# Cross network on one core: state kept as a factor, last bias added on the way to the rows, row buffer shared with the second x buffer

## The chip, the cores and the metric

The kernel runs on one core of a Trainium2 chip. The metric is the device time of one execution in microseconds; the median of three runs of the kernel before is 131.28 (131.22 to 131.41). Times inside a run come from one profiled execution and count from its span's start.

The engines that matter are TensorE (PE, matrix products into PSUM), VectorE (DVE, elementwise work), ScalarE (ACT, evictions from PSUM with a bias or as a copy) and SyncE (SP), whose in-order queue issues nearly all transfers. Each engine runs its own list of instructions in order and waits on semaphores of the others.

## The reference

```python
B, F, D, L = 4096, 26, 16, 6
Din = min(F * D, 1024)          # 416
x0: [4096, 416] bf16, ws: [6, 416, 416] bf16, bs: [6, 416] bf16

def reference(x0, ws, bs):
    x = x0
    for l in range(ws.shape[0]):
        x = x0 * (x @ ws[l] + bs[l]) + x
    return x
```

Each of the six layers multiplies the state by a 416x416 matrix, adds a bias, multiplies elementwise by the input and adds the state.

## The kernel before

The state is held transposed: features on partitions, batch rows along the free dimension. 416 features are three blocks of 128 (index k or m, tiles `XM[0]`, `XM[1]`, `XM[2]` of 128 x 3 x 4096) and a remainder of 32 (`XR[0]` to `XR[2]`, packed so that the four groups of 512 rows lie in four bands of 32 partitions). The batch is two halves, s = 0 and 1, of 2048 rows, each of four groups g of 512. `XM[0]` and `XR[0]` hold x0 through the whole kernel; the other two buffers of each kind take turns as the state read (`cur`) and written (`nxt`).

Start: x0 is loaded transposed by eight DMAs (`load_x0t`), weights and small pieces follow, and `X0rows` takes x0 again with batch rows on partitions. `bias_setup` transposes the biases into `bM` and `bR`, a value for each partition.

Layer 0 is `first_layer(s)`. Layers 1 to 4 are the loop over l: for six tiles (s, m), taken in pairs, `mm_full` and `mm_row` give a tile of 128 x 2048 in two PSUM buffers (h = 0 and 1, 1024 columns each); `rem_pair` does the remainder columns after the first pair. The elementwise work of a 128 x 1024 part is `ew_main`: ScalarE evicts with the bias (L165), VectorE multiplies by x0 (L166) and adds the old state (L169). `ew_rem` does the same with 512 columns (L173 to L175). PSUM has four buffers of two banks; `tpool` has six buffers t between ScalarE and VectorE.

The last layer (l = 5) is computed the other way round, with batch rows on partitions, so that the output is written as it lies in memory. Its products take the transposed state as the stationary operand, and its elementwise work needs x0 and the state in rows. For this, layer 4 issues DMA transposes on SyncE's queue: `xl_dmat(s, k)` right after each of its six tiles (L205, into `XLrows`), and one for each half of the remainder (L274, into `scrR`), which ScalarE then copies into `XLrows` (`xl_rem`, L278).

The last stage handles eight row blocks (`quads`) in four rounds of two; rounds 1 and 2 are s = 0, rounds 3 and 4 are s = 1. In a round TensorE makes eight units of 128 x 416: `mm_q_full` (three products a unit, L327), `mm_q_rem` (the remainder's product, L333, and the bias as a product of a row of ones with the bias row `bLr`, L336). `ew` evicts a unit or a pair of units by a copy on ScalarE (L354), multiplies by `X0rows` on VectorE (L355), and puts the pair's sum with `XLrows` off until the next call (`close_sum`, L344), after which the output transfer is issued (L345). So VectorE alternates between the product of one unit and the sum of the unit before:

```python
        tc.keep_in_program_order(nc.vector.tensor_tensor(out=tv, in0=tv, in1=X0rows[:, b, :], op=ALU.mult))
        close_sum()
        pending.append((o[:, 0:n, :], tv, XLrows[:, b, :], out_v[:, b, :], eng))
```

The order of each engine's list is settled when the program is built: the Tile scheduler may move instructions by its own estimate, except those under `keep_in_program_order`; semaphore waits are derived from which tile's region is read or written.

Of the kernel before, what the change touches and what calls it, by code (L numbers as in the profile page):

```python
# [10 lines left out]
ALU = mybir.AluOpType  # L11
# [5 lines left out]
def kernel(  # L17
# [33 lines left out]
    ones = const.tile([P, P], BF16)  # L51
# [4 lines left out]
    bLr = const.tile([P, D], BF16)  # L56
# [3 lines left out]
    XLrows = big.tile([P, NBT, D], BF16)  # L60
# [4 lines left out]
    XM = [big.tile([P, NK, B], BF16, name=f"XM{i}") for i in range(3)]  # L65
    XR = [big.tile([P, NS * CW], BF16, name=f"XR{i}") for i in range(3)]

# [29 lines left out]
    nc.gpsimd.memset(ones[:], 1.0)  # L97
# [28 lines left out]
    for g in range(NG):  # L126
        nc.sync.dma_start(bLr[32 * g:32 * g + 1, :], bs[LL:LL + 1, :])
# [18 lines left out]
    def bias_setup():  # L146
# [6 lines left out]
        nc.vector.tensor_copy(bR[:], pb[:, 3, 0:L])  # L153

# [7 lines left out]
    def ew_main(l, s, m, h, pt, cur, nxt, pin=False):  # L162
        c0 = col0(s, 2 * h)
        t = tpool.tile([P, 2 * CW], BF16, name="t")
        nc.scalar.activation(t[:], pt[:].rearrange("p a b -> p (a b)"), ACT.Identity, bias=bM[:, m, l:l + 1], scale=1.0)  # L165
        prod = nc.vector.tensor_tensor(out=t[:], in0=t[:], in1=XM[0][:, m, c0:c0 + 2 * CW], op=ALU.mult)  # L166
        if pin:
            tc.keep_in_program_order(prod)
        nc.vector.tensor_tensor(out=nxt[:, m, c0:c0 + 2 * CW], in0=t[:], in1=cur[:, m, c0:c0 + 2 * CW], op=ALU.add)  # L169

    def ew_rem(l, s, pr, curR, nxtR):
        tr = tpool.tile([P, 2 * CW], BF16, name="t")
        nc.scalar.activation(tr[:, 0:CW], pr, ACT.Identity, bias=bR[:, l:l + 1], scale=1.0)  # L173
        nc.vector.tensor_tensor(out=tr[:, 0:CW], in0=tr[:, 0:CW], in1=XR[0][:, CW * s:CW * s + CW], op=ALU.mult)  # L174
        nc.vector.tensor_tensor(out=nxtR[:, CW * s:CW * s + CW], in0=tr[:, 0:CW], in1=curR[:, CW * s:CW * s + CW], op=ALU.add)  # L175

    def mm_full(l, s, m, g, pts, cur, first, last):
        c0 = col0(s, g)
        for k in range(NK):
            for q in range(4):  # L180
                nc.tensor.matmul(pts[g // 2][32 * q:32 * q + 32, g % 2, :], lhsT=WM[:, l, k, 128 * m + 32 * q:128 * m + 32 * q + 32],  # L181
                                 rhs=cur[:, k, c0:c0 + CW], start=(first and k == 0), stop=(last and k == NK - 1),
# [8 lines left out]
    def mm_rem(l, s, pr, cur, curR):  # L191
# [3 lines left out]
        for k in range(NK):  # L195
            for g in range(NG):
                c0 = col0(s, g)
                nc.tensor.matmul(pr[32 * g:32 * g + 32, :], lhsT=WM[:, l, k, NK * P:D], rhs=cur[:, k, c0:c0 + CW],  # L198
                      start=False, stop=(k == NK - 1), tile_position=(0, 32 * g))
# [4 lines left out]
    def xl_dmat(s, k, nxt):  # L204
        nc.sync.dma_start_transpose(out=XLrows[:, 16 * s:16 * s + 16, 128 * k:128 * k + 128],  # L205
                                    in_=nxt[:, k, SW * s:SW * s + SW])

    def first_layer(s):
        cur, curR, nxt, nxtR = XM[0], XR[0], XM[1], XR[1]

        def full(pt, m, h, gl, after_row):
            c0 = col0(s, 2 * h + gl)
            for k in range(NK):
                nc.tensor.matmul(pt[:, gl, :], lhsT=WM[:, 0, k, 128 * m:128 * m + 128], rhs=cur[:, k, c0:c0 + CW],  # L214
# [30 lines left out]
        for m in range(NK):  # L245
            ew_main(0, s, m, 0, pa[m], cur, nxt)
# [11 lines left out]
        for m in range(NK):  # L258
            ew_main(0, s, m, 1, pb[m], cur, nxt, pin=(s == 0))
        ew_rem(0, s, pr[:, 0, :], curR, nxtR)  # L260
# [6 lines left out]
    def rem_pair(l, cur, curR, nxtR, feeds_last):  # L267
# [3 lines left out]
        for s in range(NS):  # L271
            ew_rem(l, s, pr2[:, s, :], curR, nxtR)
            if feeds_last:
                nc.sync.dma_start_transpose(out=scrR[s][:], in_=nxtR[:, CW * s:CW * s + CW])  # L274

    def xl_rem(s):
        tc.keep_in_program_order(
            nc.scalar.copy(XLrows[:, 16 * s:16 * s + 16, NK * P:D].rearrange("p (g i) r -> p i g r", g=NG),  # L278
                           scrR[s][:].rearrange("p i (g r) -> p i g r", g=NG)))

    cur, curR = XM[1], XR[1]
    for l in range(1, LL):
        nxt, nxtR = XM[1 + (l % 2)], XR[1 + (l % 2)]
# [129 lines left out]
```

## Time and profile before

| what | value |
| --- | --- |
| median of three runs | 131.28 us (131.22 to 131.41) |
| profiled execution: span | 128.9 us (no total of its own is given) |
| mean granted TensorE clock | 0.998 |
| layer 0, TensorE from 12.14 to 26.9 us | TensorE busy 14.86 of 14.90, VectorE 13.86, ScalarE 11.10 (12.1 to 27.0) |
| layers 1 to 4, 27.0 to 103.85 us | TensorE busy 76.85 of 76.85, VectorE 70.20, ScalarE 55.66 |
| layer 4 alone, 84.60 to 103.85 us | TensorE busy 19.25 of 19.25, VectorE 17.33, ScalarE 14.29 |
| last stage to 115.8 us (11.95 us) | TensorE busy 11.95, VectorE 10.90, ScalarE 8.50 |
| 115.8 us to the end (13.10 us) | TensorE busy 8.74, VectorE 10.10, ScalarE 7.94 |
| L165, eviction 128x1024 | 48 in layers 1 to 4, 1.115 us each |
| L166 and L169, VectorE 128x1024 | 60 each, 0.690 and 0.696 us |
| L355 and L344, VectorE 128x832 | 9 each, 0.589 and 0.584 us |
| L355 and L344, VectorE 128x416 | 14 each, 0.367 and 0.366 us |
| output transfers of 208 KB, of 104 KB | 9 and 14; 2.4 and 1.7 us from issue to landing (median) |

A busy time is the union of an engine's instructions in the stretch. Matrix products are pipelined, so a single one's duration (379 ns for 512 columns) is longer than the distance between two starts; the chain of waits gives the time that a group takes on the path.

### The profile page before, as it was taken

The numbers are of one execution on the slowest core, as the hardware profiler recorded it, in microseconds if no ns is written. First come the engines' busy times: TensorE is split into PE (matmuls) and PEld (weight loads), VectorE is DVE, ScalarE is ACT, GpSimd is POOL, SyncE is SP. The second block draws the span as 40 slices with busy tenths as digits, with TensorE's granted clock in tenths as the row PEclk, the third lists the DMA queues.
The fourth block names the chain that finished last, engine by engine and source line by source line (L and its number), as shares of the span: only waits on it lengthen the run. The fifth ranks groups of instructions, "written<-read, shape, count | busy, mean of one in ns | idle before, by whom it ended". The sixth has DMA issues, their size and how long they took to land.

```text
span 128.9 us, 3973 instructions
## 1 busy us (share of the span) xinstructions
PE 123.1 (96%) x1690; PEld 54.9 (43%) x1690; DVE 107.1 (83%) x197; ACT 86.9 (67%) x99; POOL 5.9 (5%) x18
## 2 busy tenths in 40 slices
PE   6999999999999999999999999999999999999960
PEld 2343443354444444444444444444444445445420
DVE  1032979999999898989898989898989899898991
ACT  0426783987848577848668848668847896569670
POOL 4022200600000000000000000000000000000000
PEclk9999999999999999999999999999999999999999
DMA  3999999999990000000000000000297999995754
GB/s 106 237 203 217 170 158 260 247 328 333 336 299 11 5 0 8 0 0 5 0 5 0 5 0 5 0 5 0 42 166 164 123 219 178 187 323 188 231 179 139
DMA packets 42102, 16.37 MB, mean 127 GB/s; under 512 B 30906, under 2 KB 42084, under 8 KB 42084
## 3 DMA queue, kind: packets, MB, share of 16 engines
q1 hardware_dynamic: 39416, 15.56, 54.6%
q10 hardware_dynamic: 2668, 0.56, 2.3%
q8 instruction: 13, 0.21, 0.7%
q14 instruction: 5, 0.04, 0.1%
HBM read 6.15 MB, written 3.41 MB: 74 GB/s over the span
## 4 chain that ended last, share of the span: by engine, by line
PE 80%; DMA 8%; DVE 5%; issue 2%; SPq 1%; ACT 1%; DVEq 0%
PE pt L181 49%; PE ph L214 9%; DMA XM<-in_x_dram 8%; PE py L327 8%; PE pt L187 5%; PE pr L198 5%; DVE t L355 3%; DVE o L344 2%; PE pr L193 2%; SPq L76 1%; PE py L333 1%; PE ph L221 1%; PE py L336 1%; ACT t L354 1%; PE pr L157 0%
## 5 line engine op out<-in xcount | busy, mean ns | idle before, releaser
L181 PE MATMUL pt<-XM,WM 128*32 128x512 bf16 x1152 | 65.2, 379 | 0.0
L165 ACT ACTIVATE t<-pt,bM 128x1024 bf16<-128x1024 f32 x48 | 49.6, 1115 | 18.3 <-PE pt L187 18.3
L166 DVE TENSOR_TENSOR t<-t,XM 128x1024 bf16<-128x1024 bf16 x60 | 41.4, 690 | 5.3 <-ACT t L165 5.3
L169 DVE TENSOR_TENSOR XM<-t,XM 128x1024 bf16<-128x1024 bf16 x60 | 41.8, 696 | 3.4
L181 PEld LDWEIGHTS <-WM 128*32 128x32 bf16 x1152 | 29.7, 97 | 33.8 <-issue 5.1
L354 ACT CAST t<-py 128x416 bf16<-128x416 f32 (+1 forms) x23 | 14.8, 642 | 4.8 <-PE py L327 2.1
L327 PE MATMUL py<-WM,XM 128*128 128x416 bf16 x96 | 17.7, 340 | 0.0
L214 PE MATMUL ph<-XM,WM 128*128 128x512 bf16 x72 | 16.5, 379 | 0.1
L165 ACT ACTIVATE t<-ph,bM 128x1024 bf16<-128x1024 f32 x12 | 12.5, 1114 | 4.4 <-PE ph L221 4.4
L327 PEld LDWEIGHTS <-XM 128*128 128x128 bf16 x96 | 9.0, 98 | 8.5 <-issue 1.4
L355 DVE TENSOR_TENSOR t<-t,X0rows 128x416 bf16<-128x416 bf16 (+1 forms) x23 | 10.4, 454 | 1.2 <-ACT t L354 1.2
L214 PEld LDWEIGHTS <-WM 128*128 128x128 bf16 x72 | 6.8, 98 | 8.6 <-issue 1.3
L344 DVE TENSOR_TENSOR o<-t,XLrows 128x416 bf16<-128x416 bf16 (+1 forms) x23 | 10.3, 451 | 0.0
L173 ACT ACTIVATE t<-pr,bR 128x512 bf16<-128x512 f32 x10 | 6.4, 684 | 2.7 <-PE pr L198 2.1
L198 PE MATMUL pr<-XM,WM 128*32 128x512 bf16 x120 | 8.2, 379 | 0.0
L187 PE MATMUL pt<-XR,WR 32*128 32x512 bf16 x96 | 7.3, 379 | 0.0
L141 PE MATMUL wps<-warm 128*128 128x512 bf16 (+1 forms) x11 | 4.4, 593 | 1.2 <-DVE warm L94 1.2
L175 DVE TENSOR_TENSOR XR<-t,XR 128x512 bf16<-128x512 bf16 x10 | 4.2, 423 | 0.7
L198 PEld LDWEIGHTS <-WM 128*32 128x32 bf16 x120 | 3.2, 97 | 3.1
L106 ACT ACT_TABLE_LOAD x1 | 1.3, 1283 | 4.3 <-DMA WM<-in_ws_dram 4.3
L174 DVE TENSOR_TENSOR t<-t,XR 128x512 bf16<-128x512 bf16 x10 | 4.2, 418 | 0.0
L152 DVE CAST bM<-pb 128x18 f32<-128x18 bf16 x1 | 0.2, 177 | 4.6 <-PE pb L151 4.6
(39 smaller groups left out, 33.6 us busy)
## 6 DMA issues: line engine op xcount, KB each, us to landing
X0rows<-in_x_dram SPq DMA_DIRECT2D x4, 832.0 KB, 11.6
out_dram<-o SPq DMA_DIRECT2D x9, 208.0 KB, 2.4
WM<-in_ws_dram SPq DMA_DIRECT2D x5, 312.0 KB
out_dram<-o SPq DMA_DIRECT2D x13, 104.0 KB, 1.7
WR<-in_ws_dram SPq DMA_DIRECT2D x4, 130.0 KB, 4.1
WM<-in_ws_dram ACTq DMA_DIRECT2D x1, 312.0 KB
XM<-in_x_dram SPq DMA_TRANSPOSE x8, 4.9
xrig<-in_x_dram ACTq DMA_DIRECT2D x4, 32.0 KB, 4.1
```

Source lines behind the costliest of these rows:

```text
L165: nc.scalar.activation(t[:], pt[:].rearrange("p a b -> p (a b)"), ACT.Identity, bias=bM[:, m, l:l + 1], scale=1.0)
L166: prod = nc.vector.tensor_tensor(out=t[:], in0=t[:], in1=XM[0][:, m, c0:c0 + 2 * CW], op=ALU.mult)
L169: nc.vector.tensor_tensor(out=nxt[:, m, c0:c0 + 2 * CW], in0=t[:], in1=cur[:, m, c0:c0 + 2 * CW], op=ALU.add)
L173: nc.scalar.activation(tr[:, 0:CW], pr, ACT.Identity, bias=bR[:, l:l + 1], scale=1.0)
L181: nc.tensor.matmul(pts[g // 2][32 * q:32 * q + 32, g % 2, :], lhsT=WM[:, l, k, 128 * m + 32 * q:128 * m + 32 * q + 32], rhs=cur[:, k, c0:c ...
L187: nc.tensor.matmul(pts[g // 2][:, g % 2, :], lhsT=WR[32 * g:32 * g + 32, l, 128 * m:128 * m + 128], rhs=curR[32 * g:32 * g + 32, CW * s:CW ...
L198: nc.tensor.matmul(pr[32 * g:32 * g + 32, :], lhsT=WM[:, l, k, NK * P:D], rhs=cur[:, k, c0:c0 + CW], start=False, stop=(k == NK - 1), tile ...
L214: nc.tensor.matmul(pt[:, gl, :], lhsT=WM[:, 0, k, 128 * m:128 * m + 128], rhs=cur[:, k, c0:c0 + CW], start=(k == 0 and not after_row), sto ...
L327: nc.tensor.matmul(py[:, 0:D], lhsT=cur[:, k, q_cols(q, g)], rhs=WM[:, l, k, :], start=((not closes) and k == 0), stop=(closes and k == NK ...
L344: tc.keep_in_program_order(nc.vector.tensor_tensor(out=o, in0=t, in1=xl, op=ALU.add))
L354: nc.scalar.copy(tv, src)
L355: tc.keep_in_program_order(nc.vector.tensor_tensor(out=tv, in0=tv, in1=X0rows[:, b, :], op=ALU.mult))
```

## The change

The state is kept as a factor c with x = x0 * c, so that one layer is c <- c + (x @ W + b), x <- x0 * c. The factor lies in new tiles `CM` and `CR`. In layer 0 c is 1 + (x0 @ W + b): the eviction writes it directly with a bias that has 1 added (`bias_setup`), and VectorE only multiplies. In layers 1 to 4 VectorE adds the evicted t to c and multiplies c by x0.

The rows needed by the last stage are now those of c with the last layer's bias already added: out = x0 * ((x @ W) + (c + b)). So the last stage adds the rows of c first and multiplies by `X0rows` second (`ew`, `close_out`), and the products of ones with `bLr` are gone, with `ones`, `bLr` and its four loads. The bias is added to the transposed c, in place, 1024 columns at a time: six parts on ScalarE (the set `ON_ACT`, issued by `act_bias`) and six on VectorE, the remainder's two parts on VectorE.

The rows of c are written into `shared[s]`, one tile for each half, which also serves as the second x buffer (`x2_cols`) in place of `XM[2]`. Layer 4 reads x from it. `XLrows` is gone. `cl_dmat`, the transpose into `shared[s]`, is issued for (0,0) and (0,1) after the tile (0,2), for (0,2) after the tile (1,0), for (1,0) at the end of layer 4, and for (1,1) and (1,2) in the source after the second pair of rounds 1 and 2.

In the compiled program SyncE's queue has, in this order: two remainder transposes; `shared[0]` k = 0, 1, 2; `shared[1]` k = 0, 1; four output transfers; `shared[1]` k = 2; the other output transfers. The first row addition waits for the three transposes of `shared[0]`, the first of s = 1 for the three of `shared[1]`.

```diff
-    ones = const.tile([P, P], BF16)
-    bLr = const.tile([P, D], BF16)
-    XLrows = big.tile([P, NBT, D], BF16)
-    XM = [big.tile([P, NK, B], BF16, name=f"XM{i}") for i in range(3)]
+    XM = [big.tile([P, NK, B], BF16, name=f"XM{i}") for i in range(2)]
+    CM = big.tile([P, NK, B], BF16)
+    shared = [big.tile([P, 16, D], BF16, name=f"shared{s}") for s in range(NS)]
     XR = [big.tile([P, NS * CW], BF16, name=f"XR{i}") for i in range(3)]
+    CR = big.tile([P, NS * CW], BF16)
...
+    def x2_cols(k, s, c, n):
+        return shared[s][:].rearrange("p b d -> p (b d)")[:, SW * k + c:SW * k + c + n]
+
+    XC = [x0_cols, x1_cols, x2_cols]
...
-    for g in range(NG):
-        nc.sync.dma_start(bLr[32 * g:32 * g + 1, :], bs[LL:LL + 1, :])
...
+        nc.vector.tensor_scalar_add(bM[:, :, 0:1], bM[:, :, 0:1], 1.0)
+        nc.vector.tensor_scalar_add(bR[:, 0:1], bR[:, 0:1], 1.0)
...
+    def ew_main(l, s, m, h, pt, nxt, pin=False):
         c0 = col0(s, 2 * h)
+        c = CM[:, m, c0:c0 + 2 * CW]
+        if l == 0:
+            nc.scalar.activation(c, pt[:].rearrange("p a b -> p (a b)"), ACT.Identity, bias=bM[:, m, 0:1], scale=1.0)
+        else:
+            t = tpool.tile([P, 2 * CW], BF16, name="t")
+            nc.scalar.activation(t[:], pt[:].rearrange("p a b -> p (a b)"), ACT.Identity, bias=bM[:, m, l:l + 1], scale=1.0)
+            nc.vector.tensor_tensor(out=c, in0=t[:], in1=c, op=ALU.add)
+        prod = nc.vector.tensor_tensor(out=nxt(m, s, 2 * h * CW, 2 * CW), in0=c, in1=XM[0][:, m, c0:c0 + 2 * CW], op=ALU.mult)
...
+    def add_last_bias(s, m, h, eng):
+        c0 = col0(s, 2 * h)
+        c, b = CM[:, m, c0:c0 + 2 * CW], bM[:, m, LL:L]
+        if eng is nc.scalar:
+            return nc.scalar.activation(c, c, ACT.Identity, bias=b, scale=1.0)
+        return eng.tensor_scalar_add(c, c, b)
...
+    def cl_dmat(s, k):
+        nc.sync.dma_start_transpose(out=shared[s][:, :, 128 * k:128 * k + 128], in_=CM[:, k, SW * s:SW * s + SW])
...
             if feeds_last:
-                nc.sync.dma_start_transpose(out=scrR[s][:], in_=nxtR[:, CW * s:CW * s + CW])
+                cs = slice(CW * s, CW * s + CW)
+                nc.vector.tensor_scalar_add(CR[:, cs], CR[:, cs], bR[:, LL:L])
+                nc.sync.dma_start_transpose(out=scrR[s][:], in_=CR[:, cs])
...
+    ON_ACT = {(0, 0, 0), (0, 2, 0), (0, 2, 1), (1, 0, 0), (1, 1, 0), (1, 2, 0)}
+
+    def act_bias(*units):
+        for u in units:
+            tc.keep_in_program_order(add_last_bias(*u, nc.scalar))
...
             for h in range(2):
-                ew_main(l, s, m, h, pts[t][h], cur, nxt)
-            if feeds_last:
-                xl_dmat(s, m, nxt)
+                ew_main(l, s, m, h, pts[t][h], nxt)
+                if feeds_last and (s, m, h) not in ON_ACT:
+                    add_last_bias(s, m, h, nc.vector)
...
             finish(ta)
+            if feeds_last and n == 2:
+                cl_dmat(0, 0)
+                cl_dmat(0, 1)
             for g in range(NG):
                 mm_full(l, tb[0], tb[1], g, pts[tb], cur, False, True)
             finish(tb)
+            if feeds_last and n == 0:
+                act_bias((0, 0, 0))
+            if feeds_last and n == 2:
+                act_bias((0, 2, 0), (0, 2, 1))
+                cl_dmat(0, 2)
+            if feeds_last and n == 4:
+                act_bias((1, 0, 0))
+                cl_dmat(1, 0)
...
-        for g in range(NG):
-            nc.tensor.matmul(py[g][:, 0:D], lhsT=ones[32 * g:32 * g + 1, :],
-                             rhs=bLr[32 * g:32 * g + 1, :], start=False, stop=(g < done), tile_position=(32 * g, 0))
...
-            tc.keep_in_program_order(nc.vector.tensor_tensor(out=o, in0=t, in1=xl, op=ALU.add))
+            tc.keep_in_program_order(nc.vector.tensor_tensor(out=o, in0=t, in1=xr, op=ALU.mult))
...
-        tc.keep_in_program_order(nc.vector.tensor_tensor(out=tv, in0=tv, in1=X0rows[:, b, :], op=ALU.mult))
-        close_sum()
-        pending.append((o[:, 0:n, :], tv, XLrows[:, b, :], out_v[:, b, :], eng))
+        tc.keep_in_program_order(nc.vector.tensor_tensor(out=tv, in0=tv, in1=shared[s][:, r, :], op=ALU.add))
+        close_out()
+        pending.append((o[:, 0:n, :], tv, X0rows[:, b, :], out_v[:, b, :], eng))
...
             ew(q + u // 4, u % 4, n, tiles[tl][:, a:a + n, 0:D], nc.scalar if q + 2 == NQ and u == 7 else nc.sync)
+            if q < 4 and u == 2:
+                act_bias((1, 1 + q // 2, 0))
+                cl_dmat(1, 1 + q // 2)
```

More of the change, by code (lines that the diff above doesn't have):

```diff
@@ L167, in ew_main, with ew_rem @@
         if pin:
             tc.keep_in_program_order(prod)
[L169 to L175, printed above, removed]
+    def ew_rem(l, s, pr, nxtR):
+        cs = slice(CW * s, CW * s + CW)
+        c = CR[:, cs]
+        if l == 0:
+            nc.scalar.activation(c, pr, ACT.Identity, bias=bR[:, 0:1], scale=1.0)
+        else:
+            tr = tpool.tile([P, 2 * CW], BF16, name="t")
+            nc.scalar.activation(tr[:, 0:CW], pr, ACT.Identity, bias=bR[:, l:l + 1], scale=1.0)
+            nc.vector.tensor_tensor(out=c, in0=tr[:, 0:CW], in1=c, op=ALU.add)
+        nc.vector.tensor_tensor(out=nxtR[:, cs], in0=c, in1=XR[0][:, cs], op=ALU.mult)
@@ L181, in mm_full @@
                 nc.tensor.matmul(pts[g // 2][32 * q:32 * q + 32, g % 2, :], lhsT=WM[:, l, k, 128 * m + 32 * q:128 * m + 32 * q + 32],
-                                 rhs=cur[:, k, c0:c0 + CW], start=(first and k == 0), stop=(last and k == NK - 1),
+                                 rhs=cur(k, s, CW * g, CW), start=(first and k == 0), stop=(last and k == NK - 1),
                                  tile_position=(0, 32 * q))
@@ L350, in ew @@
         b = slice(b0, b0 + 4 * (n - 1) + 1, 4)
+        r = slice(4 * g0 + i, 4 * (g0 + n - 1) + i + 1, 4)
         t = tpool.tile([P, 2 * CW], BF16, name="t")
@@ L381 @@
                 close(u - 1, 2)
-    close_sum()
+    close_out()
 _INS = ['x0', 'ws', 'bs']
```

49 lines of the change are left out of this document (20 added, 29 removed).

## The prediction

> **What bounds the kernel now.** I read the page's busy times and its chain first, then the waits and the timeline of the last 25 us.
>
> ```profile
> PE 123.1 (96%) x1690; PEld 54.9 (43%) x1690; DVE 107.1 (83%) x197; ACT 86.9 (67%) x99; POOL 5.9 (5%) x18
> PE 80%; DMA 8%; DVE 5%; issue 2%; SPq 1%; ACT 1%; DVEq 0%
> L336 PE MATMUL py<-bLr,ones 1*128 1x416 bf16 x32 | 2.8, 335 | 0.0
> ```
>
> TensorE is busy from 12.14 us, when its last input lands, to 115.6; there the chain passes to ScalarE and then VectorE until 126.04. So the five matrix layers are TensorE's, and the last stage is shared. That stage begins at 103.85 and has four rounds of two row blocks. TensorE takes 5.15 us for each of the first two rounds.
>
> VectorE reads as follows in the timeline where the second half of the batch (s=1) begins:
>
> ```profile
> 115.68 0.58 DVE L344 TENSOR_TENSOR o<-t,XLrows 128x832 bf16<-128x832 bf16 x1
> 116.69 0.59 DVE L355 TENSOR_TENSOR t<-t,X0rows 128x832 bf16<-128x832 bf16 x1 [0.43 <-ACT t L354]
> 117.20 0.58 DVE L344 TENSOR_TENSOR o<-t,XLrows 128x832 bf16<-128x832 bf16 x1
> 117.70 0.37 DVE L355 TENSOR_TENSOR t<-t,X0rows 128x416 bf16<-128x416 bf16 x1
> ```
>
> Operations on 128x832 start 0.50 apart and those on 128x416 0.29 apart. From 116.69 on VectorE waits for nothing long; its last sum ends at 126.32, 9.63 us later, and the span ends 2.6 us after that. Whatever moves the instruction of 116.69 moves the end.
>
> The third view is SyncE's queue, which issues the transposes of the last layer's state into rows:
>
> ```profile
> 98.83 1.22 SPq L274 DMA_TRANSPOSE scrR<-XR  x1
> 100.14 2.02 SPq L205 DMA_TRANSPOSE XLrows<-XM  x1
> 102.26 3.67 SPq L205 DMA_TRANSPOSE XLrows<-XM  x1
> 106.02 1.81 SPq L205 DMA_TRANSPOSE XLrows<-XM  x1
> 107.93 3.62 SPq L205 DMA_TRANSPOSE XLrows<-XM  x1
> 111.64 0.55 SPq L345 DMA_DIRECT2D out_dram<-o  x1
> ```
>
> Four transposes of 128x2048 one behind the other hold the queue for 2.02, 3.67, 1.81 and 3.62 us. By the trace's landing events they land 5.28, 5.04, 5.41 and 5.18 us after their issue began: at 105.4, 107.3, 111.4 and 113.1. The last is 3.6 us ahead of 116.69, so none is felt now.
>
> **The change, part by part.** All sums are against this execution (span 128.9; no total of its own is given). The median of the three runs, 131.28, lies 2.35 above the span, and I carry that over.
>
> *Taken from TensorE:* 32 products with ones. Four run side by side in 0.18 us in the chain (0.18 PE py L336 x4), so 8 x 0.18 = 1.44 us. Only the first two rounds' share, 0.72, lies ahead of 116.69; behind it VectorE sets the pace, not TensorE.
>
> *Taken from VectorE:* in layer 0 twelve additions of 128x1024 (0.70 each) and two of 128x512 (0.42), 9.2 us. They lie beside TensorE, which is never late for them between 12.14 and 26.9, so I price this at nothing. Were TensorE's cover gone they would be worth up to 9.2. Layers 1 to 4 keep two operations for each tile. The four loads of the bias row, issued between 31 and 35 us, have nothing behind them until 91.6: nothing. The two additions of 1 to the bias tiles stand behind casts that ended at 6.2, and ScalarE needs them at 11.09: nothing.
>
> *Added to ScalarE:* six in-place bias additions of 128x1024. The eviction of that shape from PSUM takes 1.115; 128x512 takes 0.684 from PSUM and 0.625 as a copy in SBUF, so 1.06 to 1.12. I take 1.08.
>
> *Added to VectorE:* six in-place additions of a per-partition bias on 128x1024 and two on 128x512. No such operation is in the trace. Above, it is bounded by the two-tensor operation of the same size, 0.69; below, by the one-tensor copy of half the size, 0.42 (L160, 128x512). I take 0.42, since the addition reads one tensor where the product reads two, and keep 0.69 for the range. Each delays what follows by about 0.46: 0.34 until the next start (operations overlap by 0.08) and 0.12 because it must see its predecessor end (0.73 instead of 0.61 between starts). The Trainium skill, VectorE: DVE Perf Modes (the perf-mode tier table), states that a one-source bf16 operation in SBUF runs four elements a cycle, a two-source one two. Estimated from its cycle breakdown that gives 0.43 for 1024; the 0.69 of L166 agrees with its rate for two sources, and no row here shows one source. By that page the sum stays as it is.
>
> *Moved:* the rows of the state now land in the buffer that the last matrix layer still reads. In the compiled order of SyncE's queue the two remainder transposes come first, then three transposes for s=0, two for s=1, four output transfers, and only then the last transpose for s=1. The row addition, which was the second operation of each pair, is now the first, and waits for all three transposes of its half. Behind a waiting addition stand all later VectorE operations, then the outputs on SyncE's queue, then ScalarE's evictions (six t buffers), then TensorE's banks.
>
> So the path is this.
> - Remainders: before, their first VectorE operation starts at 94.24. Three bias operations ahead of it add 3 x 0.46: 95.6. The first remainder with its bias is done at 97.0, the second transpose (1.23 us of queue each) has been issued at 99.5.
> - Five transposes back to back, at the durations of the fence, start at 99.5, 101.6, 105.3, 107.2 and 110.9; the queue is free at 112.9. What else they need is earlier: TensorE's last read of s=0 at 94.8 and of s=1 at 103.85; ScalarE's biases at 101.4, 106.9 and 110.2, counted on from its eviction that ends at 99.3.
> - The third lands at 105.3 + 5.2 = 110.5. VectorE, through with layer 4 at 107.57 before, gets there at about 109.7, because of the biases; so the first row addition starts at 110.6, **first wait** 0.9.
> - From it to the end of the fourth output product are nine operations, 8 x 0.505 + 0.58: 115.2. The fourth output transfer takes the queue for 0.45, so the last transpose is issued at 115.7. Its bias on ScalarE, behind the sixth eviction, is ready at about 115.3, so both ways agree. It lands at 115.7 + 5.2 = 120.9.
> - VectorE has finished s=0 at about 117.7 and waits 3.3, **second wait**, for the first addition of s=1 at 121.0 instead of 116.69: 4.3 later. The 9.63 behind it stay: VectorE is back to back there, and after a wait of that length its input is stocked.
>
> 131.28 + 4.3 = 135.6.
>
> **Rivals.**
> *Only ScalarE's chain holds (shorter).* If VectorE isn't late, because biases cost nearly nothing and the transposes keep out of each other's way, the last transpose still waits for its bias. The sixth eviction, at 112.18, starts at most 0.72 earlier: 111.46 + 0.85 + 1.08 = 113.4, landing 118.6, so 2.0 later: 133.2. Even with no change on ScalarE at all the transpose stands behind the fourth output, whose product ended at 112.63 before. For it: gaps of 0.2 to 0.4 in VectorE's layer 4 soak up a part. Against it: four transposes in a row did hold the queue 11 us.
> *Dearer.* Biases at 0.69 add 0.27 three times ahead of the remainders and twice more in their small form, about 1.0 in all, to 136.6; four output transfers in the same queue (2.4 us to landing each) may hold the last transpose 0.5 more: 137.1.
> *Faster.* The last stage follows TensorE: the rows of s=1 are there by 115.9 and the 0.72 arrives, 130.6. It decides if the last transpose is issued before 110.7. Four outputs stand ahead of it in the compiled order, the fourth of which went out at 113.32 before; against it by 2.6 us. A landing between 116 and 117 would be no change.
> *TensorE's clock drops.* In this trace the filler products L141 start 0.43 apart at the kernel's beginning, later products of that size 0.216. If the wait let the clock fall to that half, the last seven units, 0.54 each, would take 1.08 against VectorE's 0.575: 7 x 0.5 = 3.5 more, 139. The page shows a granted clock of 9 tenths or more in every slice; t buffers and banks let TensorE run on for about half of the 3.3, so it would idle less than 2. The Trainium skill, TensorE: Matmul & The Clock Gate (Part 1), puts the drop at an idle window of about 3.4 us; by that rule it doesn't come here, and no run yet shows an idle stretch so long.
> *That the change doesn't do what it says:* the compiled orders show the 32 products and 14 additions gone, so I leave that out.
>
> **How the numbers follow.** Forecast 135.6 with both waits: 0.60. Shorter, around 133.2: 0.19. Dearer, around 137: 0.10. Clock: 0.03. Faster: 0.05. No change: 0.03. A measurement of this kernel tells about 0.2% (0.26 us) from no change. Hence faster 0.05, same 0.03, slower 0.92. The range reaches from the shorter case, 133.0, to the bounds of the bias price and the crowded queue, 137.3; what it leaves out is the faster, same and clock cases and the edges of two others, under 0.2.
>
> **What would show it.** Right: L336 gone; layer 0 with one VectorE operation for each tile; the last transpose issued behind the fourth output near 115.7; and two idle stretches of VectorE ahead of the row addition, put down to a DMA, one near 110 and a longer one ending near 121; from there 9.6 us to the last product. Wrong: a last transpose that lands before 117, or a bias operation far from 0.42, or VectorE entering the last stage by 108.

## The result, and the profile after

The changed kernel takes 135.0 us (median of 4 runs, 134.66 to 135.24); the kernel before takes 131.25 beside it on the same chip (4 runs, 130.63 to 131.41). The ratio is 1.030, with a 95% interval of 1.0266 to 1.0334: 3.75 us slower. The profiled execution took 135.07 with a span of 133.2. One run of early_two_queues, 321.9 us long, counts as slow and is left out of its figure below.

From the profile of the changed kernel: its busy times, its chain by engine and the two new kinds of bias addition (busy us, mean ns of one, idle time before):

```profile
PE 122.6 (92%) x1656; PEld 54.7 (41%) x1658; DVE 102.1 (77%) x193; ACT 92.4 (69%) x105; POOL 4.9 (4%) x17
PE 63%; DVE 16%; DMA 8%; ACT 6%; issue 3%; SPq 1%; DVEq 0%; ACTq 0%
L200 ACT ACTIVATE CM<-CM,bM 128x1024 bf16<-128x1024 bf16 x6 | 7.0, 1159 | 0.3 <-DVE XM L181 0.2
L201 DVE TENSOR_SCALAR CM<-CM,bM 128x1024 bf16<-128x1024 bf16 x6 | 2.9, 486 | 0.2
```

VectorE has five microseconds less to do than before and the kernel is slower. The chain shows why that is no contradiction: TensorE's share fell from 80% to 63%, and VectorE's rose from 5% to 16%. The saved work lay in layer 0, beside TensorE; the added work lies at the end of layer 4, and there VectorE and ScalarE take the chain over.

The timeline of VectorE in the changed kernel, from its last bias addition to the first row addition of s = 1 (start, duration):

```profile
110.46 0.49 DVE L201 TENSOR_SCALAR CM<-CM,bM 128x1024 bf16<-128x1024 bf16 x1
110.86 1.08 DVE L390 TENSOR_TENSOR t<-t,shared 128x832 bf16<-128x832 bf16 x2
...
118.23 0.58 DVE L378 TENSOR_TENSOR o<-t,X0rows 128x832 bf16<-128x832 bf16 x1
120.62 0.59 DVE L390 TENSOR_TENSOR t<-t,shared 128x832 bf16<-128x832 bf16 x1 [1.80 <-ACT t L389]
```

The first row addition follows its predecessor without a gap, at 110.86. The first of s = 1 comes after 1.80 us of idle time. The trace puts that wait to ScalarE's casts, but the cast that this addition reads, the last on 128x832, had ended at 118.35, 2.3 us earlier. What landed at 120.54, just ahead of it, is the last transpose. SyncE's queue shows where it stood:

```profile
100.39 1.84 SPq L229 DMA_TRANSPOSE shared<-CM  x1
102.28 3.62 SPq L229 DMA_TRANSPOSE shared<-CM  x1
106.00 2.03 SPq L229 DMA_TRANSPOSE shared<-CM  x1
108.21 2.44 SPq L229 DMA_TRANSPOSE shared<-CM  x1
110.98 2.02 SPq L229 DMA_TRANSPOSE shared<-CM  x1
113.09 2.77 SPq L379 DMA_DIRECT2D out_dram<-o  x4
115.97 3.17 SPq L229 DMA_TRANSPOSE shared<-CM  x1
```

Five transposes, four outputs, and then the last transpose at 115.97, which is 8.0 us later than the last one of the kernel before (107.93). VectorE's last product ends at 130.20 (126.32 before) and the span 3.0 us behind that (2.6 before).

### The profile page after: what moved, and what is told of

It is laid out like the page before. It is cut to its first block, busy times and chain, and to the rows that moved or that the text cites. A ratio compares the mean times of both kernels' runs of the same rounds, so it can differ in the third digit from the quotient of the medians.

```text
span 133.2 us, 3894 instructions
## 1 busy us (share of the span) xinstructions
PE 122.6 (92%) x1656; PEld 54.7 (41%) x1658; DVE 102.1 (77%) x193; ACT 92.4 (69%) x105; POOL 4.9 (4%) x17
## 4 chain that ended last, share of the span: by engine, by line
PE 63%; DVE 16%; DMA 8%; ACT 6%; issue 3%; SPq 1%; DVEq 0%; ACTq 0%
PE pt L206 38%; PE ph L236 8%; DMA XM<-in_x_dram 8%; PE py L364 6%; DVE XM L181 5%; DVE CM L180 4%; PE pt L212 4%; PE pr L222 4%; ACT t L389 3%; DVE t L390 3%; ACT CM L200 1%; PE pr L218 1%; DVE CM L201 1%; SPq L87 1%; DVE o L378 1%
## 5 line engine op out<-in xcount | busy, mean ns | idle before, releaser
L180 DVE TENSOR_TENSOR CM<-t,CM 128x1024 bf16<-128x1024 bf16 x48 | 32.9, 686 | 4.9 <-ACT t L179 4.9
L206 PE MATMUL pt<-shared,WM 128*32 128x512 bf16 x576 | 32.9, 379 | 0.0
L206 PE MATMUL pt<-XM,WM 128*32 128x512 bf16 x576 | 32.9, 379 | 0.0
L181 DVE TENSOR_TENSOR XM<-CM,XM 128x1024 bf16<-128x1024 bf16 x36 | 24.8, 694 | 8.4 <-ACT CM L176 6.6
L181 DVE TENSOR_TENSOR shared<-CM,XM 128x1024 bf16<-128x1024 bf16 x24 | 16.6, 692 | 1.3
L176 ACT ACTIVATE CM<-ph,bM 128x1024 bf16<-128x1024 f32 x12 | 12.5, 1114 | 4.5 <-PE ph L243 4.5
L390 DVE TENSOR_TENSOR t<-t,shared 128x416 bf16<-128x416 bf16 (+1 forms) x23 | 10.3, 451 | 2.1 <-ACT t L389 2.1
L378 DVE TENSOR_TENSOR o<-t,X0rows 128x416 bf16<-128x416 bf16 (+1 forms) x23 | 10.3, 449 | 0.0
L200 ACT ACTIVATE CM<-CM,bM 128x1024 bf16<-128x1024 bf16 x6 | 7.0, 1159 | 0.3 <-DVE XM L181 0.2
L194 DVE TENSOR_TENSOR XR<-CR,XR 128x512 bf16<-128x512 bf16 x10 | 4.2, 423 | 0.6
```

The lines of the kernel that those rows point to most:

```text
L176: nc.scalar.activation(c, pt[:].rearrange("p a b -> p (a b)"), ACT.Identity, bias=bM[:, m, 0:1], scale=1.0)
L180: nc.vector.tensor_tensor(out=c, in0=t[:], in1=c, op=ALU.add)
L181: prod = nc.vector.tensor_tensor(out=nxt(m, s, 2 * h * CW, 2 * CW), in0=c, in1=XM[0][:, m, c0:c0 + 2 * CW], op=ALU.mult)
L378: tc.keep_in_program_order(nc.vector.tensor_tensor(out=o, in0=t, in1=xr, op=ALU.mult))
```

## The experiments

A kernel is given by its per cent above the kernel before, measured beside it on the same chip (130.7 to 131.0 us there, 131.25 beside the changed kernel). Times inside a kernel are from its profile. "First of s=1" is VectorE's first row addition of the second half, "end" the end of its last product, "tail" from there to the span's end.

| kernel | above before, 95% | enters last stage | first of s=1 | end | tail |
|---|---|---|---|---|---|
| before | 0 | 107.57 | 116.69 | 126.32 | 2.6 |
| changed | 3.0 (2.7 to 3.3) | 110.86 | 120.62 | 130.20 | 3.0 |
| bias_by_products | -0.1 (-0.3 to 0.1) | 107.28 | 116.39 | 126.04 | 2.6 |
| no_last_bias | 0.35 (0.0 to 0.7) | 107.31 | 115.56 | 125.19 | 4.2 |
| no_bias_four_outputs_less | -0.7 (-0.9 to -0.5) | 107.35 | 115.60 | 125.18 | 2.6 |
| no_bias_own_buffer | 0.65 (0.4 to 0.9) | 107.39 | 115.63 | 126.44 | 3.1 |
| no_bias_own_in_place | -0.2 (-0.5 to 0.05) | 108.11 | 116.35 | 125.94 | 3.1 |
| late_transpose_alone | 1.3 (0.9 to 1.7) | 107.92 | 118.12 | 127.71 | 3.2 |
| early_transpose | 2.0 (1.5 to 2.5) | 111.34 | 118.87 | 128.45 | 3.8 |
| early_two_queues | 2.1 (1.7 to 2.5) | 111.83 | 119.36 | 128.95 | 3.4 |
| bias_added_own_buffer | 3.25 (2.9 to 3.6) | 111.21 | 119.45 | 130.05 | 3.0 |
| bias_added_own_in_place | 1.8 (1.55 to 2.1) | 111.39 | 118.92 | 128.50 | 3.0 |
| late_transpose_no_act_bias | 5.5 (4.9 to 6.2) | 111.53 | 121.49 | 131.28 | 3.3 |
| bias_on_gpsimd | 10.8 (10.3 to 11.3) | 112.06 | 129.36 | 139.2 | 3.2 |

The profiles differ from their start: TensorE's first product of the last stage begins between 103.48 us (bias_by_products) and 104.44 (early_two_queues), at 103.78 in the kernel before and at 104.19 in the changed one, because TensorE waited up to 0.7 us for the last input in some of them. The columns of times contain that difference.

**What does the change cost without its bias additions?** The bias goes back to products with ones; factor form and shared buffer stay. All six transposes stand ahead of the outputs, since they no longer wait for a bias.

```diff
+            nc.tensor.matmul(py[g][:, 0:D], lhsT=ones[32 * g:32 * g + 1, :], rhs=bLr[32 * g:32 * g + 1, :], ...
-                nc.vector.tensor_scalar_add(CR[:, cs], CR[:, cs], bR[:, LL:L])
-                if feeds_last and (s, m, h) not in ON_ACT:
-                    add_last_bias(s, m, h, nc.vector)
-            tc.keep_in_program_order(add_last_bias(*u, nc.scalar))
```

> The changed kernel with the 32 products with ones put back for the last bias, and every addition of the last bias to the factor left out; the rows still share the second x buffer, and all six transposes are now ready ahead of the first output. Theory (two halves: VectorE's and ScalarE's bias additions make VectorE enter the last stage about 3 us late, and the last transpose, issued behind four outputs, holds the first row addition of the second half): both halves go, so about 131.3, as the kernel before; the first row addition of the second half starts near 116.8. Rival A (sharing the buffer is what costs, since rows can't land before layer 4 has read it): 134 or more, with VectorE idle before the first row addition of each half. Rival B (keeping the state as a factor costs in layers 1 to 4): the slowdown stays at 135.

It came out at 130.73 beside 130.74. So, taken together, the rest of the change costs no time: the shared buffer, the form x0 * c and the later start of the transposes (97.0 instead of 91.6). And the 9.2 us of VectorE saved in layer 0 bring nothing. Nor does a gain hide a cost in the layers between: TensorE is busy 57.00 of the 57 us from 27 to 84 in both kernels.

**What would a bias that costs nothing be worth?** The same, with the last bias left out altogether: no products, and the additions taken out as in the diff above.

> The changed kernel with the last layer's bias left out altogether: no products with ones, no additions to the factor, so the output lacks that bias. Theory: the time if the bias were free. TensorE is 1.44 us shorter, of which 0.72 to 0.9 arrives because VectorE sets the pace of the last two rounds: 130.4. Rival A (sharing costs): 134 or more. Rival C (the whole 1.44 arrives): 129.8.

This missed. VectorE did end earlier, at 125.19 instead of 126.04, but the time did not fall. Its output transfers, the page's group of DMA issues (count, KB each, us to landing):

```profile
out_dram<-o SPq DMA_DIRECT2D x9, 208.0 KB, 2.7
out_dram<-o SPq DMA_DIRECT2D x13, 104.0 KB, 2.3
out_dram<-o ACTq DMA_DIRECT2D x1, 104.0 KB, 2.4
```

Before, these were 2.4 and 1.7 us. The first output went out at 113.37, behind the sixth transpose, when products had been ready since 109; SyncE held one issue for 1.37 us, and its last issue ended 1.5 us after VectorE had finished. To see whether these transfers really set the end, four of them were left out:

```diff
-            eng.dma_start(dst, o)
+            if len(sent) >= 4:
+                eng.dma_start(dst, o)
+            sent.append(1)
```

> Leaves out the last bias, as no_last_bias did, and also the first four output transfers (208 KB each, 0.83 of 3.41 MB). VectorE, ScalarE and TensorE do the same work as in no_last_bias. Theory: with the shared buffer the transposes end at 113 us, the outputs start behind them, and from there the output transfers, not VectorE, set the end; with four fewer the distance from VectorE's last product to the span's end falls from 4.2 us to about 2.5, as in the kernel before, and the time is about 1.0 under the kernel before (no_last_bias was 0.6 above it): 129.8. Rival (the tail of 4.2 us has nothing to do with the transfers ahead of it): 131.3, as without this edit.

```profile
out_dram<-o SPq DMA_DIRECT2D x13, 104.0 KB, 1.8
out_dram<-o SPq DMA_DIRECT2D x5, 208.0 KB, 2.2
out_dram<-o ACTq DMA_DIRECT2D x1, 104.0 KB, 1.8
```

VectorE ended at the same time (125.18), the landings took 1.8 and 2.2 us, and the tail went from 4.2 to 2.6: 129.8, as forecast. So without any cost for the bias, the output transfers behind six transposes are the next bound. With this order of the queue the products with ones, 0.72 us ahead of the second half, were nearly free: they stood in time that the outputs need anyway. The bound isn't a fixed time: bias_by_products, with the same order, issued its first output at 113.12 and ended at 128.6, earlier than no_last_bias at 129.4, whose runs scatter from 130.29 to 132.08. Why its transfers took longer at the end is not shown.

**Does a buffer of its own change that?** With a separate row buffer, and the transposes issued earlier in the source, the first transposes go out at 90.7 and the outputs at 109.8. Five output tiles in place of ten made room for it.

```diff
-    opool = ctx.enter_context(tc.tile_pool(name="opool", bufs=10))
+    opool = ctx.enter_context(tc.tile_pool(name="opool", bufs=5))
-    XM = [big.tile([P, NK, B], BF16, name=f"XM{i}") for i in range(2)]
+    XM = [big.tile([P, NK, B], BF16, name=f"XM{i}") for i in range(3)]
...
-        return shared[s][:].rearrange("p b d -> p (b d)")[:, SW * k + c:SW * k + c + n]
+        return XM[2][:, k, SW * s + c:SW * s + c + n]
```

> Leaves out the last bias; the row buffer is separate from the second x buffer (five output tiles in place of ten make room for it), and the first two transposes go out as early as in the kernel before. Theory: transposes end near 110 us, outputs start at 111 to 112 as in the kernel before, so the output transfers no longer set the end and the 0.84 us that VectorE gains without the products with ones arrives: 0.7 to 1.0 under the kernel before, near 129.9. Rival (free bias is worth nothing with any buffer, because outputs take their time in all cases): within 0.3 of the kernel before. Rival (five output tiles hold VectorE up, as a tile comes free only when its transfer has landed): 132 or more, with VectorE waiting for DMA ahead of L376's products.

```profile
DVE o L375 <- DMA out_dram<-o: 1.1, 1, 1.1
```

This is the waits of VectorE by what it waited for (us in total, times, longest): one wait of 1.1 us for an output tile whose transfer had not landed, the third case of the expectation, though the time, 131.50 beside 130.81, stayed short of its 132. So this kernel says nothing of the buffer. Written in place, the product needs no output tile:

```diff
-        o = opool.tile([P, 2, D], BF16, name="o")
-        pending.append((o[:, 0:n, :], tv, X0rows[:, b, :], out_v[:, b, :], eng))
+        pending.append((X0rows[:, b, :], tv, X0rows[:, b, :], out_v[:, b, :], eng))
```

> Leaves out the last bias. As no_bias_own_buffer, but the last product is written back over the rows of x0 that it reads, so that no output tile has to come free (there VectorE waited 1.07 us for one of the five). Theory: VectorE's end goes back to 125.2, the tail to about 2.5, since the outputs start at 110 to 112: 129.8 to 130.1, 0.8 under the kernel before. Rival (outputs take their time in any order, so a free bias buys nothing): 130.7 or more. Rival (writing in place slows VectorE's product): its rows of 0.37 and 0.58 grow.

130.77 beside 131.01, and an interval that reaches just over no change. The expected 0.8 did not come; 0.2 did, at most 0.65. The wait is gone. In this profile VectorE entered the last stage 0.8 later than in no_last_bias, and the tail was 3.1 instead of 2.5. The 0.8 comes from the start of the execution, as TensorE's timeline in layer 0 shows:

```profile
12.68 3.40 PE L235 MATMUL ph<-XM,WM 128*128 128x512 bf16 x15 [0.66 <-DMA XM<-in_x_dram]
```

TensorE waited 0.66 us for the last input, which no_last_bias did not, and its last stage began at 104.31 instead of 103.52. Counted from there VectorE ends at 125.15, where 125.2 was expected. The longer tail, which takes most of that gain back, was not tracked to a cause, so why a free bias would be worth so little here is only in part explained.

**What do the bias additions cost by themselves?** Here the bias is added again, four parts by ScalarE and eight by VectorE, with nothing else in the way: own buffer, all transposes ahead of the outputs, products in place. The kernel with five output tiles came first.

> The changed kernel with a separate row buffer (five output tiles), the first two transposes as early as in the kernel before, and all transposes ahead of the outputs; the bias is still added to the transposed factor, by ScalarE for four tiles and by VectorE for the others. Theory: VectorE still enters the last stage at about 110.8 because of its own additions, its end is about 128.4 as in early_transpose, but the outputs find the queue emptier: 132.3 to 132.8 (early_transpose: 133.5). If sharing the buffer were the main cost: 131 or less. If sharing costs nothing even with the additions: 133.4.

> The changed kernel with a row buffer of its own, all transposes ahead of the outputs, four ScalarE biases, and the product written in place, so that neither the shared buffer nor the number of output tiles holds anything. What is left against the kernel before is the bias additions alone. Theory: VectorE enters the last stage at about 111.3 instead of 107.57, needs 0.84 less for it on the way, ends at 128.4 to 128.6 with a tail of 2.5 to 3.0: 2.0 to 2.4 above the kernel before, 132.8 to 133.2. If the additions alone are cheap and the changed kernel's time is the queue's: 131.5 or less.

The first is spoiled as above (two waits for output tiles, 1.5 us in all) and gave 3.25%. The second gave 1.8%: 133.25 beside 131.01. VectorE never waits in its last stage, yet enters it at 111.39 instead of 107.57 and ends 2.2 later than before. Its timeline, at the entry:

```profile
111.39 1.08 DVE L389 TENSOR_TENSOR t<-t,shared 128x832 bf16<-128x832 bf16 x2
...
118.92 0.58 DVE L389 TENSOR_TENSOR t<-t,shared 128x832 bf16<-128x832 bf16 x1
```

From the first addition to the first of s = 1 it needs 7.5 us, against 9.1 in the kernel before: by then its input is stocked, and it gives part of the delay back. That is why an entry 3.8 us late costs 2.2. The products with ones are gone here too, as in the changed kernel, so this is the price of the additions less whatever those products cost.

**What does the late transpose cost by itself?** No bias, and the last transpose fixed behind four outputs, as it stands in the changed kernel.

```diff
+            if q == 2 and u == 0:
+                tc.keep_in_program_order(nc.sync.dma_start_transpose(out=shared[1][:, :, 256:384], in_=CM[:, 2, SW:2 * SW]))
```

> The last layer's bias left out as in the run without it, but the last transpose of the second half held behind the first four outputs, as the changed kernel has it; so no bias work, only the late transpose. Theory: fourth output near 112.9, transpose issued near 113.4, landed near 118.2, first row addition of the second half at 118.3 instead of 116.7 in the kernel before and near 116 without the delay: 132.5 to 132.9, about 2.3 above the run without bias. Rival D (bias work makes all of the loss and the transpose's lateness is only cover for it): 130.4, as without the delay.

```profile
118.12 0.59 DVE L387 TENSOR_TENSOR t<-t,shared 128x832 bf16<-128x832 bf16 x1 [2.20 <-ACT t L386]
```

VectorE's timeline shows the wait, 2.20 us, again put down to ScalarE. The last transpose had landed at 118.04. The kernel is 1.3% slower than before (medians 132.63 and 130.74): the queue's half of the prediction's shorter rival, without any bias. The opposite edit leaves the additions in and puts the last two transposes ahead of the outputs, with their two ScalarE biases moved to VectorE:

```diff
-    ON_ACT = {(0, 0, 0), (0, 2, 0), (0, 2, 1), (1, 0, 0), (1, 1, 0), (1, 2, 0)}
+    ON_ACT = {(0, 0, 0), (0, 2, 0), (0, 2, 1), (1, 0, 0)}
                 cl_dmat(1, 0)
+                cl_dmat(1, 1)
+                cl_dmat(1, 2)
...
-                cl_dmat(1, 1 + q // 2)
```

> The changed kernel with the last two transposes of the second half issued at the end of layer 4, ahead of all outputs; their two ScalarE bias additions move to VectorE, all twelve parts and the remainder still get the bias. Theory: the late transpose's part goes (about 1.9 us of waiting in the changed kernel's trace), the part of the bias work stays: the first row addition of the second half starts near 118.9 without a wait for a transfer, 133.2. Rival D (bias work alone): 135 or more, as two more additions lie on VectorE. Rival E (the transpose alone): 131.3 or less.

The wait is gone, VectorE ends 1.75 earlier than in the changed kernel, and the time is 2.0% above before instead of 3.0%. Part of the gain is lost again in a tail of 3.8 us.

**Is that tail SyncE's queue or the transfers themselves?**

```diff
-            ew(..., nc.scalar if q + 2 == NQ and u == 7 else nc.sync)
...
+            ew(..., nc.scalar if q + 2 == NQ and u == 7 else (nc.sync, nc.gpsimd)[count[0] % 2])
+            count[0] += 1
```

> early_transpose (133.5, tail of 3.8 us behind VectorE's end) with every second output transfer issued by GpSimd instead of SyncE. Nothing else changes. If the tail is the length of the outputs' queue on SyncE (one issue each 0.48 us when it lags), it falls to about 2.6 and the time to 132.3. If it is the DMA engines themselves that are full, both queues share them and the time stays at 133.3 to 133.6. If GpSimd's issues cost VectorE something: 134 or more, with longer rows on VectorE.

```profile
out_dram<-o SPq DMA_DIRECT2D x5, 208.0 KB, 4.4
out_dram<-o POOLq DMA_DIRECT2D x4, 208.0 KB, 4.4
```

Two queues, and each large output takes 4.4 us to land, where one queue took 3.4. The time is 2.1% above before, the same as with one queue. A second queue doesn't help. The outputs start against full DMA engines, which both queues share: their busy share is 1.0 or more from 108 to 120 us in both kernels. From 126 us on it is below 0.75, though. So SyncE's queue is not what makes the tail; what does is not shown.

**Queue or ScalarE?** In the changed kernel the last transpose could have waited for the fourth output in the queue (out at 115.86) or for its own bias on ScalarE (done at 115.95). Here both late ScalarE biases are on VectorE, by the smaller `ON_ACT` of early_transpose, and the last transpose is fixed behind four outputs, by the line of late_transpose_alone:

> The changed kernel with two of ScalarE's biases, for (1,1,0) and (1,2,0), moved to VectorE, and SyncE's queue in exactly its order: four outputs ahead of the last transpose. In the changed kernel that transpose was issued at 115.97 us, when the fourth output had left the queue (115.86) and ScalarE's bias had just ended (115.95), so either could have held it. If the queue alone does it: VectorE enters the last stage about 0.5 later than in the changed kernel (110.86), the fourth output and the transpose move with it to 116.3 to 116.6, the wait stays at 1.5 to 2, and the time is 3.0 to 3.6 per cent above the kernel before: 135.0 to 135.7. If ScalarE's late bias is what holds it: the wait goes, and the time is that of early_transpose, 2.0 per cent above: 133.5.

The transpose was issued at 116.58, right behind the fourth output (116.15, held for 0.37), and landed at 121.41:

```profile
121.49 0.59 DVE L391 TENSOR_TENSOR t<-t,shared 128x832 bf16<-128x832 bf16 x1 [2.35 <-issue]
...
130.62 0.66 DVE L379 TENSOR_TENSOR o<-t,X0rows 128x416 bf16<-128x416 bf16 x2
```

VectorE waited 2.35 us. So the queue's order alone is enough. But the time was well above the expected 135.0 to 135.7: the four runs took 136.39, 137.43, 137.83 and 139.24, which is 4.2 to 6.4% above the 130.91 beside them (their median 5.1%). The shortest is the profiled one. TensorE's timeline, and its rows in the table by stretches (stretch; us; busy of PE, PEld, DVE, ACT, POOL; granted clock; DMA share; GB/s):

```profile
120.50 0.35 PE L371 MATMUL py<-WR,XR 32*128 32x416 bf16 x2
123.23 0.35 PE L371 MATMUL py<-WR,XR 32*128 32x416 bf16 x2 [2.38 <-ACT t L390]
124.02 0.54 PE L371 MATMUL py<-WR,XR 32*128 32x416 bf16 x4 [0.44 <-ACT t L390]
```

```profile
120.00:124.00 4.00, 1.20 (x8) 0.29 (x6) 2.51 (x7) 1.01 (x2) 0.00 (x0) 0.95 0.76 225
124.00:128.00 4.00, 3.98 (x17) 1.78 (x17) 3.98 (x14) 2.01 (x4) 0.00 (x0) 0.62 0.72 223
```

TensorE stood idle for 2.38 us, and then its clock was granted at half, from 123.6 to 127.0 us in finer stretches. So the event that the prediction's clock rival names does occur, a small edit away from the changed kernel. Its price in this profile is small, though: from the first addition of s = 1 to the last product VectorE takes 9.79 us, against 9.58 in the changed kernel, because it works on stocked input until about 127. The profiled run is 1.3 us longer than the changed kernel's (136.39, 135.07) mainly because the first addition of s = 1 comes 0.87 later. What made the other three runs 1.0 to 2.9 us longer still isn't shown: they have no trace. Their mean granted clocks, 0.984, 0.975 and 0.965 beside 0.984 in the profiled run, are lower in two of them only.

In the changed kernel ScalarE's evictions run later, TensorE works until 121.93 and the transpose lands 0.87 earlier, so TensorE's idle stretches are 0.43 each; its clock stays at 1.00 to the end of its work.

**GpSimd instead of VectorE and ScalarE.**

```diff
-                    add_last_bias(s, m, h, nc.vector)
+                    add_last_bias(s, m, h, nc.gpsimd)
```

Ten of the twelve parts go to GpSimd and two stay on ScalarE; the remainder's two stay on VectorE, and all transposes stand ahead of the outputs.

> The shared buffer, with the bias additions of VectorE and of all but two ScalarE tiles moved to GpSimd, all transposes ahead of the outputs; the two remainder additions stay on VectorE. No row shows such an addition on GpSimd. If one takes 1.5 us or less and disturbs nobody, VectorE enters the last stage near 108 and the outputs set the end as in no_last_bias: 131.3 to 132. If GpSimd takes 2 us or more for one, the transposes of s=1 are late, and VectorE waits for them: 134 or more. If its operations slow VectorE's down, VectorE's rows of 0.69 grow while GpSimd is busy.

```profile
L201 POOL TENSOR_SCALAR CM<-CM,bM 128x1024 bf16<-128x1024 bf16 x10 | 32.8, 3292 | 65.6 <-DVE XM L181 65.6
```

```profile
129.36 0.59 DVE L391 TENSOR_TENSOR t<-t,shared 128x832 bf16<-128x832 bf16 x1 [7.16 <-DMA shared<-CM]
```

```profile
98.21 3.39 POOL L201 TENSOR_SCALAR CM<-CM,bM 128x1024 bf16<-128x1024 bf16 x1
99.01 1.41 DVE L181 TENSOR_TENSOR XM<-CM,XM 128x1024 bf16<-128x1024 bf16 x1
100.34 0.68 DVE L180 TENSOR_TENSOR CM<-t,CM 128x1024 bf16<-128x1024 bf16 x1
101.05 0.69 DVE L181 TENSOR_TENSOR XM<-CM,XM 128x1024 bf16<-128x1024 bf16 x1
```

One addition takes 3.29 us on GpSimd, ten take 33, and the last transposes are late by so much that VectorE waits 7.2 us for them (second fence). The third fence is from the timelines of GpSimd and VectorE in that kernel: a multiplication takes 1.41 instead of 0.69 while GpSimd works, and the two operations behind it take their usual time beside the same GpSimd addition. This repeats: beside each of the first nine GpSimd additions one VectorE operation, which starts 0.45 to 0.87 us after it, takes 0.65 to 0.84 longer, be it a multiplication, a row addition or a product of the last stage. Apart from one small bias addition the others beside them aren't lengthened. Why it is that one is not shown. TensorE stood idle for 7.77 us here, and its clock was at half from 124.7 to 135.0; VectorE's last part took 9.82 us all the same.

None of these kernels beats the one before by more than the measurement tells apart while it computes the bias.

## Why the prediction was right, step by step

The forecast was 135.6, the measurement 135.0. The step that carries it held: the last transpose behind four outputs delays the first row addition of s = 1 by about four microseconds. The first of the two waits did not exist, and that the sum came so close is in part luck: sizes that were off nearly cancel.

- **TensorE's 32 products at 0.72, VectorE's 14 additions of layer 0 at nothing.** The second is shown by bias_by_products: they are gone, and the time is that of before. The first is no term of the 4.3, but the faster rival rests on it, and it was too much: with the bias left out the time did not fall by 0.72, but rose 0.6 with the shared buffer, where the outputs then set the end, and fell 0.2 with a buffer of its own, where the cause is open.
- **Bias on ScalarE at 1.08:** measured 1.16, above the bounds of 1.06 to 1.12 and slower than the eviction of that shape from PSUM, 1.115.
- **Bias on VectorE at 0.42:** measured 0.49 on 128x1024, in the lower part of the range of 0.42 to 0.69, and 0.35 on 128x512. Estimated from the Trainium skill, VectorE: DVE Perf Modes (the perf-mode tier table), one-source operations at four elements a cycle would take 0.43; the trace bears out the faster rate for one source (0.69 for two), with 0.06 more on it. Each addition delays the next operation by 0.52 where 0.46 was forecast. The lower bound of 0.42 came from a copy that reads PSUM (L160) and bounds nothing of an addition in SBUF: the same half size took 0.35 there. That 0.42 came near is luck.
- **Start of five transposes at 99.5, 101.6, 105.3, 107.2 and 110.9, queue free at 112.9:** measured 100.39, 102.28, 106.00, 108.21, 110.98, and 113.1. The first is 0.9 late, of which 0.4 was there when TensorE began (12.55 instead of 12.14, as its last input landed later).
- **First wait of 0.9 ahead of the first row addition: this step failed.** VectorE was forecast there at 109.7 and the third transpose at 110.5. The transpose landed at 110.44; VectorE arrived at 110.86 and did not wait at all. The mis-sized term is VectorE's own delay: 2.1 us in the forecast, 3.3 measured (2.9 without the late start). The prediction does not work the 2.1 out; its own 0.46 for each of six additions already makes 2.8. In the trace the six make 3.1 and the two small ones 0.4, and gaps of 0.6 in the kernel before take part of it up. The first row addition came at 110.86 instead of 110.6, so the sum hardly moved: the delay too short and the wait that did not come cancelled, which is luck. One of the two idle stretches that the prediction names as signs of being right is therefore missing.
- **Last transpose issued at 115.7, landing at 120.9:** issued at 115.97, behind the fourth output (out at 115.86) and its own bias (done at 115.95); landed at 120.54, since it took 4.57 us and not 5.2. late_transpose_no_act_bias shows that the queue's order is enough to hold it.
- **Second wait of 3.3:** 1.8 measured. VectorE was through with s = 0 at 118.8 instead of 117.7, since it began later and waited 0.26 for an eviction at 116.72; and the landing was 0.4 earlier.
- **First addition of s = 1 at 121.0, and 9.63 behind it:** 120.62, and 9.58. The step that carried the forecast held.
- **The rest of the sum.** 3.9 us at the first addition of s = 1 and 0.4 more in the tail make the 4.3 between the spans. The forecast had all 4.3 ahead of that addition and nothing in the tail, so that the spans agree with it is luck. The median is 3.75 above: time and span of the profiled execution differ by 1.9 here, where 2.35 was carried over.
- **The rivals.** The queue's half of the shorter one was real as a mechanism: 1.3% with the late transpose alone. Additions alone are 1.8%. Together 3.1%, against 3.0% measured, so the two parts add up about. The sum is not exact: both kernels lack the products with ones, whose removal it counts twice (between 0.35% more and 0.2% less in the runs without a bias), and the second has a buffer of its own. The faster rival failed because the transpose did stand behind the outputs, as the prediction held against it; and with the transposes early the outputs themselves take the gain, which was not in the prediction. The clock rival did not come in the changed kernel, but in one with the same queue; there the half clock cost VectorE 0.2 us in the profiled run, where the prediction priced it at 3.5.

## What to carry to other kernels

Work taken out beside a busy engine bought nothing here, and a small operation moved from the busiest engine to the hand-over between two stages can cost more than it saves: ask what the receiving engine is late for. In one in-order DMA queue, the position of a transfer that the next stage needs counts as well as the work that feeds it: one transpose moved ahead of four outputs was worth a per cent, beside 1.8% for the additions. When a saving does not arrive, look at the tail behind the last engine: the transfers may have been the second bound all along.

## What the runs showed of the hardware that was not expected

- TensorE's clock halved (0.50 granted, from 123.6 to 127.0 us) after an idle stretch of 2.38 us and 0.35 us of work. The Trainium skill, TensorE: Matmul & The Clock Gate (Part 1), puts the drop at an idle window of about 3.4 us, which runs freely and does not begin with the idle time. The length of the slow stretch, 3.4 us, agrees; but the drop came although TensorE had worked for about 1 us within the 3.4 us ahead of it. An idle stretch shorter than the window isn't safe by this run. An idle stretch of 7.77 us in bias_on_gpsimd was followed by 10.2 us at 0.50. In both kernels VectorE, with its input stocked, needed only 0.2 us more for its last part (9.79 and 9.82 instead of 9.58).
- A 208 KB output takes 2.2 to 2.4 us to land with room, and longer behind six transposes: 2.7 in no_last_bias, 3.4 in early_transpose, 3.8 in bias_by_products, 4.4 from two queues at once. A long landing isn't a loss by itself: bias_by_products took the time of the kernel before, with the same tail of 2.6.
- GpSimd needs 3.29 us for an in-place bias addition that takes 0.49 on VectorE and 1.16 on ScalarE, and each of the first nine such additions lengthened one VectorE operation beside it (a multiplication of 128x1024 from 0.69 to 1.41) and left nearly all others as they were.
